# A decode kernel with w_in loaded ahead of wq, narrower moving columns at the end, and the last two rows of wo loaded 8 partitions at a time

## The chip, the cores and the metric

The kernel runs on one NeuronCore of a Trainium2 chip. The metric is device time in microseconds (us), the median of several executions. "Span" is the time from the first to the last instruction in one profiled execution; it is about 2 us shorter than the device time. Ratios are computed as the mean time of one kernel's fast runs over the mean time of the other's fast runs of the same rounds, so they are not quite the ratio of the medians quoted beside them.

Engines are named as the profile names them: PE is TensorE, PEld its weight loads, DVE VectorE, ACT ScalarE, SP SyncE. SPq and ACTq are the instruction streams of SP and ACT when they issue a DMA.

## The reference, cut to what matters

One token (x of 1024 values) goes through two blocks that are mixed by a gate:

```python
g = sigmoid((x * gate_w).sum(-1))
# A: attention of 32 query heads over 4 cached K/V heads, 65536 positions, head size 128
q = (x @ wq)                              # wq: 1024 x 4096
p = softmax(q . k_cache * 128 ** -0.5)    # k_cache, v_cache: 4 x 65536 x 128 bf16, 67 MB each
a = (p . v_cache) @ wo                    # wo: 4096 x 1024
# B: gated MLP
z = gelu(x @ w_in)                        # w_in: 1024 x 3584
b = (z1 * (w_sp * layernorm(z2) + b_sp)) @ w_out   # w_out: 1792 x 1024
out = g * a + (1 - g) * b
```

All told 162 MB are read for 2 KB of output, so this is first of all a streaming kernel.

## The kernel before: the parts that matter

Every big load goes through one helper and one pool of five 32 KB-per-partition buffers, issued by SyncE in program order. A load of a 6th tile has to wait until TensorE has finished with the tile five loads earlier.

```python
NKV = 5
WO_SPLIT = (16, 8, 4, 2, 2)     # wo's 32 row groups of 256 KB, in five loads
W = 64                          # moving columns of most score and V matmuls
WL = 128                        # moving columns of the last V group and of out_ps
...
kv = ctx.enter_context(tc.tile_pool(name="kv", bufs=NKV))
def load(src, shape, name):
    t = kv.tile([P, CT * P], BF16, name=name, tag="kv")
    ...
    nc.sync.dma_start(out=v, in_=src)
    return v
```

The order of the loads is wq (2), then K and V tiles of four heads alternating (16 + 12), then w_in's first half, V, w_in's second half, V, V, V, w_out, and wo in five pieces. The tail of the program is:

```python
z_part(0)                       # x @ w_in, first half: 112 matmuls of 18 columns
last_v(0)                       # V of the last head, tile 0: 128 matmuls of WL columns
z_part(1)
...                             # gelu, layernorm, gate: small DVE/ACT work
for j in range(1, NT):
    last_v(j)
...
def project(src, n, vec, c0, name, first=False, last=False):
    w = load(src, (n, D), name)
    for c in range(n):
        for j in range(NJ):     # NJ = 8 output blocks of 128
            nc.tensor.matmul(out_ps[j // NB][:, j % NB, :], lhsT=w[:, c, j * P:(j + 1) * P],
                             rhs=vec[:, c0 + c:c0 + c + 1].to_broadcast([P, WL]), ...)
project(B_w_out..., FC, uT, 0, "wout_t", first=True)
for n in WO_SPLIT:
    project(wo_view[:, c0:c0 + n, :], n, oa, c0, "wo_t", last=(c0 + n == OC))
    c0 += n
...                             # copy, transpose, cast, store of 2 KB
```

Moving columns are those of the operand that streams through TensorE: at full clock a matmul with 128 of them takes about 59 ns here. Only 8 of them are wanted in the scores and V matmuls (the heads of a group) and one in out_ps. The others are neighbours or copies whose products nobody reads, so their number is free.

Of the kernel before, what the change touches and what calls it, by code (L numbers as in the profile page):

```python
# [7 lines left out]
FP32 = mybir.dt.float32  # L8
BF16 = mybir.dt.bfloat16
I32 = mybir.dt.int32  # L10
ACT = mybir.ActivationFunctionType
ALU = mybir.AluOpType
AX = mybir.AxisListType

P = 128
# [3 lines left out]
CPS = 64  # L19
LAG = 4  # L20
EVAC_PAT = "vav"
WO_SPLIT = (16, 8, 4, 2, 2)
SW = 256
W = 64
WL = 128


@with_exitstack
def kernel(
# [15 lines left out]
    nc = tc.nc  # L45

    _, _, D = A_x.shape
    _, G, S, DH = A_k_cache.shape
# [3 lines left out]
    F = B_w_in.shape[1]  # L52
    FH = F // 2
    KC = D // P
    FC = FH // P
    OC = HD // P
    NJ = D // P
    QD = P // H
    NCG = S // P
    NT = NCG // CT  # L60
    SCALE = float(DH) ** -0.5
    assert DH == P and D % P == 0 and FH % P == 0 and P % H == 0
    assert S % (P * CT) == 0 and CT % CPS == 0 and CPS % TG == 0 and sum(WO_SPLIT) == OC

    const = ctx.enter_context(tc.tile_pool(name="const", bufs=1))
    wk = ctx.enter_context(tc.tile_pool(name="wk", bufs=2))
# [4 lines left out]
    pss = ctx.enter_context(tc.tile_pool(name="pss", bufs=2, space=bass.MemoryType.PSUM))  # L71
    psm = ctx.enter_context(tc.tile_pool(name="psm", bufs=1, space=bass.MemoryType.PSUM))
    pso = ctx.enter_context(tc.tile_pool(name="pso", bufs=1, space=bass.MemoryType.PSUM))


    def load(src, shape, name):
        t = kv.tile([P, CT * P], BF16, name=name, tag="kv")
        n = 1
        for s in shape:
            n *= s  # L80
        v = t[:, :n]
        if len(shape) == 2:
            v = v.rearrange("p (a b) -> p a b", b=shape[1])
        nc.sync.dma_start(out=v, in_=src)  # L84
        return v

    def load_kv(src, g, j, name):
# [9 lines left out]
    nc.scalar.dma_start(out=wb[:, 0:1], in_=B_w_sp)  # L97
    nc.scalar.dma_start(out=wb[:, 1:2], in_=B_b_sp.unsqueeze(0))

    wq_view = A_wq.rearrange("(p c) n -> p c n", c=KC)  # L100
    KH = KC // 2
    wq_t = [load(wq_view[:, i * KH:(i + 1) * KH, :], (KH, HD), "wq_t") for i in range(2)]


# [8 lines left out]
    ones_f = const.tile([P, P], FP32, name="ones_f")  # L113
# [4 lines left out]
                            op0=ALU.bitwise_and)  # L118
    nc.vector.tensor_scalar(out=pbits[:, 1:2], in0=pidx[:], scalar1=OC - 1, scalar2=None,
                            op0=ALU.bitwise_and)  # L120
    nc.vector.tensor_scalar(out=pbits[:, 2:3], in0=pidx[:], scalar1=OC.bit_length() - 1,
                            scalar2=None, op0=ALU.logical_shift_right)
# [4 lines left out]
    def one_hot(shape, dtype, in0, col, name):  # L127
# [17 lines left out]
                     start=True, stop=True)  # L145
    xm = const.tile([P, 2, KC, P // KC], FP32, name="xm")
    for t in range(2):
        nc.vector.tensor_tensor(
            out=xm[:, t], in0=xb_ps[:, t * P:(t + 1) * P].rearrange("p (i c) -> p c i", c=KC),
            in1=sel_i[:].unsqueeze(1).to_broadcast([P, KC, P // KC]), op=ALU.mult)  # L150
    xa = const.tile([P, 2, KC], FP32, name="xa")
    nc.vector.tensor_reduce(out=xa[:], in_=xm[:], axis=AX.X, op=ALU.add)
    xT = const.tile([P, KC], BF16, name="xT")
# [14 lines left out]
                            op0=ALU.add)  # L168
    nc.vector.reciprocal(out=gw[:, 2:3], in_=gw[:, 1:2])
    nc.vector.tensor_scalar(out=gw[:, 5:6], in0=gw[:, 2:3], scalar1=-1.0, scalar2=1.0,  # L170
                            op0=ALU.mult, op1=ALU.add)
    gate, wsp, bsp, gate1 = gw[:, 2:3], gw[:, 3:4], gw[:, 4:5], gw[:, 5:6]


    q_ps = psm.tile([P, H], FP32, name="q_ps", tag="m")
    for c in range(KC):
        w = wq_t[c // KH]
        for h in range(H):
            nc.tensor.matmul(  # L179
                q_ps[:, h:h + 1], lhsT=w[:, c % KH, h * DH:(h + 1) * DH], rhs=xT[:, c:c + 1],  # L180
                start=(c == 0 and h == 0), stop=(c == KC - 1), skip_group_check=True,
# [9 lines left out]
    scT, mxr, spt, o_ps, s_ps = {}, {}, {}, {}, {}  # L191
# [140 lines left out]
    while steps:  # L332
        run_step()


    win_view = B_w_in.rearrange("(p c) n -> p c n", c=KC)
    zw = 512 // (2 * FC)
    z_ps = psm.tile([P, 2 * FC, zw], FP32, name="z_ps", tag="m")

    def z_part(i):  # L340
        t = load(win_view[:, i * KH:(i + 1) * KH, :], (KH, F), "win_t")
        for c in range(KH):
            w = t[:, c, :].rearrange("p (h m f) -> p h f m", h=2, f=FC)
            for hf in range(2):
                for f in range(FC):
                    nc.tensor.matmul(  # L346
                        z_ps[:, hf * FC + f, :], lhsT=w[:, hf, f, :],
                        rhs=xT[:, i * KH + c:i * KH + c + 1].to_broadcast([P, zw]),
                        start=(i == 0 and c == 0 and hf == 0 and f == 0),
                        stop=(i == 1 and c == KH - 1), skip_group_check=True)  # L350

    def last_v(j):
        rest(v_units(G - 1, j, load_kv(A_v_cache, G - 1, j, "vt")))

    z_part(0)
    last_v(0)
    z_part(1)
    z = wk.tile([P, 2 * FC], FP32, name="z")
    nc.vector.tensor_copy(out=z[:], in_=z_ps[:, :, 0])  # L359
    gt = wk.tile([P, 2 * FC], FP32, name="gt")  # L360
    nc.vector.tensor_tensor(out=gt[:], in0=z[:], in1=z[:], op=ALU.mult)
    nc.vector.tensor_scalar(out=gt[:], in0=gt[:], scalar1=0.044715, scalar2=1.0,
                            op0=ALU.mult, op1=ALU.add)
    nc.vector.tensor_tensor(out=gt[:], in0=gt[:], in1=z[:], op=ALU.mult)
    th = wk.tile([P, 2 * FC], FP32, name="th")
    nc.scalar.activation(out=th[:], in_=gt[:], func=ACT.Tanh, scale=0.7978845608028654)
    nc.vector.tensor_scalar(out=th[:], in0=th[:], scalar1=0.5, scalar2=0.5,
                            op0=ALU.mult, op1=ALU.add)
    zg = wk.tile([P, 2 * FC], FP32, name="zg")
    nc.vector.tensor_tensor(out=zg[:], in0=z[:], in1=th[:], op=ALU.mult)  # L370
    z2 = zg[:, FC:2 * FC]
    z2sq = wk.tile([P, FC], FP32, name="z2sq")
    nc.vector.tensor_tensor(out=z2sq[:], in0=z2, in1=z2, op=ALU.mult)
    rs = wk.tile([P, 2], FP32, name="rs")
    nc.vector.reduce_sum(out=rs[:, 0:1], in_=z2, axis=AX.X)
    nc.vector.reduce_sum(out=rs[:, 1:2], in_=z2sq[:], axis=AX.X)
    tot_ps = psm.tile([P, 2], FP32, name="tot_ps", tag="m")
    nc.tensor.matmul(tot_ps[:], lhsT=ones_f[:], rhs=rs[:], start=True, stop=True)
    stat = wk.tile([P, 8], FP32, name="stat")
    nc.vector.tensor_scalar(out=stat[:, 0:2], in0=tot_ps[:], scalar1=1.0 / float(FH),  # L380
                            scalar2=None, op0=ALU.mult)
    nc.vector.tensor_tensor(out=stat[:, 2:3], in0=stat[:, 0:1], in1=stat[:, 0:1], op=ALU.mult)
    nc.vector.tensor_tensor(out=stat[:, 3:4], in0=stat[:, 1:2], in1=stat[:, 2:3],
                            op=ALU.subtract)
    nc.vector.tensor_scalar(out=stat[:, 4:5], in0=stat[:, 3:4], scalar1=1e-5, scalar2=None,
                            op0=ALU.add)
    nc.scalar.activation(out=stat[:, 5:6], in_=stat[:, 4:5], func=ACT.Sqrt)
    nc.vector.reciprocal(out=stat[:, 6:7], in_=stat[:, 5:6])
    z2n = wk.tile([P, FC], FP32, name="z2n")
    nc.vector.tensor_scalar(out=z2n[:], in0=z2, scalar1=stat[:, 0:1], scalar2=stat[:, 6:7],  # L390
                            op0=ALU.subtract, op1=ALU.mult)
    nc.vector.tensor_scalar(out=z2n[:], in0=z2n[:], scalar1=wsp, scalar2=bsp,
                            op0=ALU.mult, op1=ALU.add)
    uT = const.tile([P, FC], BF16, name="uT")
    nc.vector.scalar_tensor_tensor(out=uT[:], in0=zg[:, 0:FC], scalar=gate1, in1=z2n[:],
                                   op0=ALU.mult, op1=ALU.mult)
    for j in range(1, NT):
        last_v(j)


    NB = 512 // WL
    out_ps = [pss.tile([P, NB, WL], FP32, name="out_ps", tag="spt") for _ in range(NJ // NB)]

    def project(src, n, vec, c0, name, first=False, last=False):
        w = load(src, (n, D), name)
        for c in range(n):
            for j in range(NJ):
                nc.tensor.matmul(  # L408
                    out_ps[j // NB][:, j % NB, :], lhsT=w[:, c, j * P:(j + 1) * P],
                    rhs=vec[:, c0 + c:c0 + c + 1].to_broadcast([P, WL]),  # L410
                    start=(first and c == 0 and j % NB == 0), stop=(last and c == n - 1),
                    skip_group_check=True)


# [2 lines left out]
                     rhs=ones_f[0:1, 0:1], start=True, stop=True, skip_group_check=True)  # L417
    nc.tensor.matmul(om_ps[:, :OC], lhsT=lm[:].rearrange("p h q -> p (h q)"), rhs=sel_c[:],
                     start=False, stop=True, skip_group_check=True)
    rl = wk.tile([P, 1], FP32, name="rl")  # L420
    nc.vector.reciprocal(out=rl[:], in_=om_ps[:, OC:])
    oa = const.tile([P, OC], BF16, name="oa")
    nc.vector.tensor_scalar(out=oa[:], in0=om_ps[:, :OC], scalar1=rl[:, 0:1], scalar2=gate,
                            op0=ALU.mult, op1=ALU.mult)

    project(B_w_out.rearrange("(p c) n -> p c n", c=FC), FC, uT, 0, "wout_t", first=True)
    wo_view = A_wo.rearrange("(p c) n -> p c n", c=OC)
    c0 = 0
    for n in WO_SPLIT:
        project(wo_view[:, c0:c0 + n, :], n, oa, c0, "wo_t", last=(c0 + n == OC))  # L430
        c0 += n
    out_sb = const.tile([P, NJ], FP32, name="out_sb")
    for i, t in enumerate(out_ps):
        nc.vector.tensor_copy(out=out_sb[:, i * NB:(i + 1) * NB], in_=t[:, :, 0])  # L434
    outT_ps = psm.tile([NJ, P], FP32, name="outT_ps", tag="m")
    nc.tensor.transpose(outT_ps[:], out_sb[:], ident_f[:])
    outT = const.tile([NJ, P], BF16, name="outT")
# [4 lines left out]
    last = {}  # L442
# [37 lines left out]
```

## Time and profile before

| | before |
|---|---|
| median of 3 (later 4) runs | 398.57 us (398.07) |
| span of the profiled run | 396.6 us |
| bytes read | 162.0 MB |
| TensorE's last out_ps matmul ends | 393.4 us |

The page's strip of 40 equal slices of the span (9.9 us each; digits are busy tenths, PEclk is the granted TensorE clock, GB/s what the DMA engines moved):

```profile
PE   0435999778788787878888688896987789799997
PEclk9999999999999999999999999999999977789999
DMA  8999999999999999999999999999999999999960
GB/s 357 435 423 421 425 444 433 431 423 422 428 423 408 426 414 438 426 421 416 428 440 433 431 423 422 433 425 440 433 419 430 428 431 428 438 433 423 416 259 7
```

Up to slice 38 the DMA engines are busy all the time at about 428 GB/s, and 162 MB at that rate take 378 us. In the last quarter the clock falls for some slices, while the 18-column matmuls of z_part run and shortly after, and the PE row stands at nine up to the last slice but one.

The end of the timeline of TensorE and of what follows it (columns: start us, duration us, engine, line, operation, output<-inputs, shape, count, and in brackets the idle time before and what ended it):

```profile
337.11 6.84 PE L346 MATMUL z_ps<-xT,win_t 128*128 128x18 bf16 x112
...
351.80 1.95 PE L297 MATMUL o_ps<-scT,vt 128*128 128x128 bf16 x32
...
372.17 6.63 PE L408 MATMUL out_ps<-uT,wout_t 128*128 128x128 bf16 x112
378.63 14.96 PE L408 MATMUL out_ps<-oa,wo_t 128*128 128x128 bf16 x256
393.40 0.39 DVE L434 COPY out_sb<-out_ps 128x4 f32<-128x4 f32 x2 [20.52 <-PE out_ps L408]
394.47 0.36 SPq L439 DMA_DIRECT2D out_dram<-outT  x1
```

No wait stands in brackets on the matmul lines: the projections run back to back, 59 ns per matmul, up to 393.4 us. The DMA engines stop earlier, as the windows view of the same stretch shows (first column the stretch, then busy us of PE, PEld, DVE, ACT and POOL, then clock, DMA share and GB/s):

```profile
372.00:376.00 4.00, 4.00 (x69) 4.00 (x70) 0.48 (x2) 0.00 (x0) 0.00 (x0) 1.00 0.99 422
376.00:380.00 4.00, 4.00 (x73) 4.00 (x71) 0.00 (x0) 0.00 (x0) 0.00 (x0) 1.00 0.84 337
380.00:384.00 4.00, 4.00 (x73) 4.00 (x71) 0.00 (x0) 0.00 (x0) 0.00 (x0) 1.00 0.67 266
384.00:388.00 4.00, 4.00 (x72) 4.00 (x70) 0.00 (x0) 0.00 (x0) 0.00 (x0) 1.00 0.33 132
388.00:392.00 4.00, 4.00 (x73) 4.00 (x71) 0.00 (x0) 0.00 (x0) 0.00 (x0) 1.00 0.02 4
```

The DMA share falls from about 378 us on and is near zero from 388 us: the 16 engines do not end together. So the last 6 us belong to TensorE, and behind them, at 387 us plus about 4 us of landing and epilogue, a second limit waits: the last load.

### The profile page before, as it was taken

The page shows a single profiled execution, that of the slowest core. Times are in us where ns is not written, and L with a number is a line of the kernel's source. Part 1 is how long each engine was busy: PE and PEld are TensorE (multiplying, and loading weights), DVE is VectorE, ACT ScalarE, POOL GpSimd, SP SyncE. Part 2 cuts the span into 40 slices and gives each one's busy share as a digit, 9 for nine tenths or more (in the row PEclk, how much of TensorE's full clock was granted, in tenths as well). Part 3 has the DMA queues.
Part 4 walks back from the last instruction along what each step waited for, and adds up shares of the span by engine and source line. Part 5 has one row for each costly group of instructions (what it writes and reads, how often), then busy time and mean ns, then how long its engine had stood idle before and what let it go on. Part 6 is the DMA issues. An engine that isn't in the chain of part 4 may idle for free.

```text
span 396.6 us, 14958 instructions
## 1 busy us (share of the span) xinstructions
PE 316.6 (80%) x7080; PEld 309.1 (78%) x7080; DVE 152.7 (38%) x297; ACT 121.1 (31%) x138; POOL 1.0 (0%) x9
## 2 busy tenths in 40 slices
PE   0435999778788787878888688896987789799997
PEld 0435989777788787777878687786977689799896
DVE  2002666649344444654334346643444420110100
ACT  1002555446433233436333233553333130100000
POOL 1000000000000000000000000000000000000000
PEclk9999999999999999999999999999999977789999
DMA  8999999999999999999999999999999999999960
GB/s 357 435 423 421 425 444 433 431 423 422 428 423 408 426 414 438 426 421 416 428 440 433 431 423 422 433 425 440 433 419 430 428 431 428 438 433 423 416 259 7
DMA packets 6161, 162.96 MB, mean 411 GB/s; under 512 B 724, under 2 KB 724, under 8 KB 980
## 3 DMA queue, kind: packets, MB, share of 16 engines
q1 hardware_dynamic: 6064, 162.01, 95.7%
q8 instruction: 55, 0.90, 0.8%
q14 instruction: 6, 0.05, 0.0%
q10 hardware_dynamic: 36, 0.00, 0.0%
HBM read 162.01 MB, written 0.00 MB: 409 GB/s over the span
## 4 chain that ended last, share of the span: by engine, by line
PE 71%; DMA 13%; issue 11%; ACT 3%; DVE 1%; SPq 0%; ACTq 0%
PE tps L264 27%; PE o_ps L297 18%; PE spt L243 14%; DMA kn<-in_A_k_cache_dram 13%; PE out_ps L408 5%; PE z_ps L346 3%; PE o_ps L286 2%; ACT ktt L267 1%; ACT scT L230 1%; ACT scT L249 1%; PE nb_ps L221 0%; DVE mxr L206 0%; DVE mxr L251 0%; SPq L84 0%; DVE mx L209 0%
## 5 line engine op out<-in xcount | busy, mean ns | idle before, releaser
L264 PE MATMUL tps<-ident_b,kn 128*128 128x128 bf16 x2048 | 160.2, 222 | 19.4 <-issue 10.4
L269 DVE COPY ktt<-tps 128x1024 bf16<-128x1024 bf16 x171 | 116.8, 690 | 122.4 <-PE tps L264 122.0
L264 PEld LDWEIGHTS <-kn 128*128 128x128 bf16 x2048 | 121.9, 99 | 20.7 <-issue 13.1
L267 ACT COPY ktt<-tps 128x1024 bf16<-128x1024 bf16 x85 | 85.9, 1012 | 157.8 <-PE tps L264 157.7
L297 PE MATMUL o_ps<-scT,vt 128*128 128x64 bf16 (+1 forms) x2048 | 110.4, 203 | 14.3 <-issue 14.3
L243 PE MATMUL spt<-qT,ktt 128*128 128x64 bf16 (+7 forms) x2048 | 102.9, 192 | 17.9 <-issue 16.5
L297 PEld LDWEIGHTS <-vt 128*128 128x128 bf16 x2048 | 94.9, 100 | 16.1 <-issue 15.2
L243 PEld LDWEIGHTS <-ktt 128*128 128x128 bf16 x2048 | 84.8, 98 | 20.6 <-issue 18.7
L249 ACT CAST scT<-spt 128x512 bf16<-128x512 f32 x32 | 18.9, 589 | 24.0 <-PE spt L243 14.1
L230 ACT ACTIVATE scT<-scT 128x1024 bf16<-128x1024 bf16 x16 | 16.4, 1058 | 7.5 <-DVE scT L226 7.5
L286 PE MATMUL o_ps<-scT,ones_b 128*128 128x256 bf16 x64 | 17.8, 279 | 0.4 <-DVE ssum L308 0.3
L251 DVE TENSOR_TENSOR mxr<-scT,mxr 128x512 bf16<-128x512 bf16 x24 | 10.2, 425 | 16.5 <-ACT scT L249 15.0
L346 PE MATMUL z_ps<-xT,win_t 128*128 128x18 bf16 x224 | 13.8, 206 | 1.5 <-issue 1.5
L408 PE MATMUL out_ps<-oa,wo_t 128*128 128x128 bf16 x256 | 15.0, 219 | 0.0
L408 PEld LDWEIGHTS <-wo_t 128*128 128x128 bf16 x256 | 14.8, 98 | 0.0
L346 PEld LDWEIGHTS <-win_t 128*128 128x128 bf16 x224 | 13.7, 161 | 1.5 <-issue 1.5
L179 PE MATMUL q_ps<-xT,wq_t 128*128 128x1 bf16 x256 | 7.1, 165 | 6.9 <-DMA wq_t<-in_A_wq_dram 6.4
L179 PEld LDWEIGHTS <-wq_t 128*128 128x128 bf16 x256 | 7.1, 104 | 7.0 <-DMA wq_t<-in_A_wq_dram 6.5
L226 DVE TENSOR_TENSOR scT<-scT,negm 128x1024 bf16<-128x1024 bf16 x16 | 10.7, 685 | 0.1
L359 DVE COPY z<-z_ps 128x28 f32<-128x28 f32 x1 | 0.2, 188 | 24.4 <-PE z_ps L346 24.4
L303 DVE TENSOR_TENSOR lm<-sel_q,o_ps 128x32 f32<-128x32 f32 x4 | 0.7, 182 | 22.1 <-PE o_ps L297 22.1
L434 DVE COPY out_sb<-out_ps 128x4 f32<-128x4 f32 x2 | 0.3, 162 | 20.6 <-PE out_ps L408 20.5
(85 smaller groups left out, 52.6 us busy)
## 6 DMA issues: line engine op xcount, KB each, us to landing
kn<-in_A_k_cache_dram SPq DMA_DIRECT2D x16, 4096.0 KB, 43.2
vt<-in_A_v_cache_dram SPq DMA_DIRECT2D x16, 4096.0 KB, 27.2
wq_t<-in_A_wq_dram SPq DMA_DIRECT2D x2, 4096.0 KB, 17.4
win_t<-in_B_w_in_dram SPq DMA_DIRECT2D x2, 3584.0 KB
wo_t<-in_A_wo_dram SPq DMA_DIRECT2D x1, 4096.0 KB, 33.9
wout_t<-in_B_w_out_dram SPq DMA_DIRECT2D x1, 3584.0 KB
wo_t<-in_A_wo_dram SPq DMA_DIRECT2D x1, 2048.0 KB
wo_t<-in_A_wo_dram SPq DMA_DIRECT2D x1, 1024.0 KB
```

What stands on the lines that cost most here:

```text
L179: nc.tensor.matmul(q_ps[:, h:h + 1], lhsT=w[:, c % KH, h * DH:(h + 1) * DH], rhs=xT[:, c:c + 1], start=(c == 0 and h == 0), stop=(c == KC ...
L226: nc.vector.tensor_tensor(out=blk, in0=blk, in1=negm[:].unsqueeze(1).to_broadcast([P, CT, REP]), op=ALU.add)
L230: nc.scalar.activation(out=blk, in_=blk, func=ACT.Exp, scale=SCALE)
L243: nc.tensor.matmul(spt[g][:, o:o + n], lhsT=ktt[:, j * P:(j + 1) * P], rhs=qT[:, g * REP:g * REP + n], start=True, stop=True, skip_group_c ...
L249: nc.scalar.copy(out=blk, in_=spt[g][:].rearrange("p (c h) -> p c h", h=REP))
L264: nc.tensor.transpose(tps[:, i * P:(i + 1) * P], kn[:, u * TG + i, :], ident_b[:])
L267: nc.scalar.copy(out=ktt[:], in_=tps[:])
L269: nc.vector.tensor_copy(out=ktt[:], in_=tps[:])
L286: nc.tensor.matmul(o_ps[g][:, 2 * WL:], lhsT=ones_b[:], rhs=scT[g][:, j * CT + c:j * CT + c + SW // REP, :].rearrange("p c h -> p (c h)"), ...
L297: nc.tensor.matmul(o_ps[g][:, o0:o0 + wv], lhsT=vt[:, c, :], rhs=scT[g][:, lo:hi, :].rearrange("p c h -> p (c h)"), start=False, stop=(cg ...
L346: nc.tensor.matmul(z_ps[:, hf * FC + f, :], lhsT=w[:, hf, f, :], rhs=xT[:, i * KH + c:i * KH + c + 1].to_broadcast([P, zw]), start=(i == 0 ...
L408: nc.tensor.matmul(out_ps[j // NB][:, j % NB, :], lhsT=w[:, c, j * P:(j + 1) * P], rhs=vec[:, c0 + c:c0 + c + 1].to_broadcast([P, WL]), st ...
```

## The change

Its intent: put z_part where TensorE waits for loads anyway; make the tail's matmuls shorter (V of the last head 128 to 96 columns, out_ps 128 to 64); and split wo finer at the end, with the last two rows loaded in pieces of 8 partitions. The diff, cut to its core (the z_part code is only moved, which is marked):

```diff
-WO_SPLIT = (16, 8, 4, 2, 2)
+WO_SPLIT = (16, 8, 4, 1, 1, 1, 1)
+NARROW = 2
+NB = 8
-WL = 128
+WL = 96
-    def load(src, shape, name):
+    def load(src, shape, name, nb=P):
-        nc.sync.dma_start(out=v, in_=src)
+        for p0 in range(0, P, nb):
+            nc.sync.dma_start(out=v[p0:p0 + nb], in_=src[p0:p0 + nb])
+    win_t = [load(win_view[:, i * KH:(i + 1) * KH, :], (KH, F), "win_t") for i in range(2)]
     wq_view = A_wq.rearrange("(p c) n -> p c n", c=KC)
     ...
+    z_part(0)          # and z_part(1) and the chain to uT: moved here, ahead of q,
+    z_part(1)          # from the tail
     ...
-    out_ps = [pss.tile([P, NB, WL], FP32, name="out_ps", tag="spt") for _ in range(NJ // NB)]
+    out_ps = pss.tile([P, NJ, W], FP32, name="out_ps", tag="spt")
     ...
-                    rhs=vec[:, c0 + c:c0 + c + 1].to_broadcast([P, WL]),
+                    rhs=vec[:, c0 + c:c0 + c + 1].to_broadcast([P, W]),
     ...
-    for n in WO_SPLIT:
-        project(wo_view[:, c0:c0 + n, :], n, oa, c0, "wo_t", last=(c0 + n == OC))
+    for i, n in enumerate(WO_SPLIT):
+        project(wo_view[:, c0:c0 + n, :], n, oa, c0, "wo_t", last=(c0 + n == OC),
+                nb=NB if i >= len(WO_SPLIT) - NARROW else P)
```

More of the change, by code (lines that the diff above doesn't have):

```diff
@@ L98 @@
     nc.scalar.dma_start(out=wb[:, 1:2], in_=B_b_sp.unsqueeze(0))
+    KH = KC // 2
+    win_view = B_w_in.rearrange("(p c) n -> p c n", c=KC)
+    win_t = [load(win_view[:, i * KH:(i + 1) * KH, :], (KH, F), "win_t") for i in range(2)]
     wq_view = A_wq.rearrange("(p c) n -> p c n", c=KC)
-    KH = KC // 2
     wq_t = [load(wq_view[:, i * KH:(i + 1) * KH, :], (KH, HD), "wq_t") for i in range(2)]
@@ L172, with z_part @@
     gate, wsp, bsp, gate1 = gw[:, 2:3], gw[:, 3:4], gw[:, 4:5], gw[:, 5:6]
+    zw = 512 // (2 * FC)
+    z_ps = psm.tile([P, 2 * FC, zw], FP32, name="z_ps", tag="m")
+    def z_part(i):
+        for c in range(KH):
+            w = win_t[i][:, c, :].rearrange("p (h m f) -> p h f m", h=2, f=FC)
+            for hf in range(2):
+                for f in range(FC):
+                    nc.tensor.matmul(
+                        z_ps[:, hf * FC + f, :], lhsT=w[:, hf, f, :],
+                        rhs=xT[:, i * KH + c:i * KH + c + 1].to_broadcast([P, zw]),
+                        start=(i == 0 and c == 0 and hf == 0 and f == 0),
+                        stop=(i == 1 and c == KH - 1), skip_group_check=True)
@@ new lines @@
+    z_part(0)
+    z_part(1)
+    z = wk.tile([P, 2 * FC], FP32, name="z")
+    nc.vector.tensor_copy(out=z[:], in_=z_ps[:, :, 0])
+    gt = wk.tile([P, 2 * FC], FP32, name="gt")
+    nc.vector.tensor_tensor(out=gt[:], in0=z[:], in1=z[:], op=ALU.mult)
+    nc.vector.tensor_scalar(out=gt[:], in0=gt[:], scalar1=0.044715, scalar2=1.0,
+                            op0=ALU.mult, op1=ALU.add)
+    nc.vector.tensor_tensor(out=gt[:], in0=gt[:], in1=z[:], op=ALU.mult)
+    th = wk.tile([P, 2 * FC], FP32, name="th")
@@ new lines @@
+    nc.scalar.activation(out=th[:], in_=gt[:], func=ACT.Tanh, scale=0.7978845608028654)
+    nc.vector.tensor_scalar(out=th[:], in0=th[:], scalar1=0.5, scalar2=0.5,
+                            op0=ALU.mult, op1=ALU.add)
+    zg = wk.tile([P, 2 * FC], FP32, name="zg")
+    nc.vector.tensor_tensor(out=zg[:], in0=z[:], in1=th[:], op=ALU.mult)
+    z2 = zg[:, FC:2 * FC]
+    z2sq = wk.tile([P, FC], FP32, name="z2sq")
+    nc.vector.tensor_tensor(out=z2sq[:], in0=z2, in1=z2, op=ALU.mult)
+    rs = wk.tile([P, 2], FP32, name="rs")
@@ new lines @@
+    nc.vector.reduce_sum(out=rs[:, 0:1], in_=z2, axis=AX.X)
+    nc.vector.reduce_sum(out=rs[:, 1:2], in_=z2sq[:], axis=AX.X)
+    tot_ps = psm.tile([P, 2], FP32, name="tot_ps", tag="m")
+    nc.tensor.matmul(tot_ps[:], lhsT=ones_f[:], rhs=rs[:], start=True, stop=True)
+    stat = wk.tile([P, 8], FP32, name="stat")
+    nc.vector.tensor_scalar(out=stat[:, 0:2], in0=tot_ps[:], scalar1=1.0 / float(FH),
+                            scalar2=None, op0=ALU.mult)
+    nc.vector.tensor_tensor(out=stat[:, 2:3], in0=stat[:, 0:1], in1=stat[:, 0:1], op=ALU.mult)
@@ new lines @@
+    nc.vector.tensor_tensor(out=stat[:, 3:4], in0=stat[:, 1:2], in1=stat[:, 2:3],
+                            op=ALU.subtract)
+    nc.vector.tensor_scalar(out=stat[:, 4:5], in0=stat[:, 3:4], scalar1=1e-5, scalar2=None,
+                            op0=ALU.add)
+    nc.scalar.activation(out=stat[:, 5:6], in_=stat[:, 4:5], func=ACT.Sqrt)
+    nc.vector.reciprocal(out=stat[:, 6:7], in_=stat[:, 5:6])
+    z2n = wk.tile([P, FC], FP32, name="z2n")
+    nc.vector.tensor_scalar(out=z2n[:], in0=z2, scalar1=stat[:, 0:1], scalar2=stat[:, 6:7],
+                            op0=ALU.subtract, op1=ALU.mult)
@@ L175 @@
+    nc.vector.tensor_scalar(out=z2n[:], in0=z2n[:], scalar1=wsp, scalar2=bsp,
+                            op0=ALU.mult, op1=ALU.add)
+    uT = const.tile([P, FC], BF16, name="uT")
+    nc.vector.scalar_tensor_tensor(out=uT[:], in0=zg[:, 0:FC], scalar=gate1, in1=z2n[:],
+                                   op0=ALU.mult, op1=ALU.mult)
     q_ps = psm.tile([P, H], FP32, name="q_ps", tag="m")
@@ L333 @@
         run_step()
-    win_view = B_w_in.rearrange("(p c) n -> p c n", c=KC)
-    zw = 512 // (2 * FC)
-    z_ps = psm.tile([P, 2 * FC, zw], FP32, name="z_ps", tag="m")
-    def z_part(i):
-        t = load(win_view[:, i * KH:(i + 1) * KH, :], (KH, F), "win_t")
-        for c in range(KH):
-            w = t[:, c, :].rearrange("p (h m f) -> p h f m", h=2, f=FC)
-            for hf in range(2):
-                for f in range(FC):
-                    nc.tensor.matmul(
-                        z_ps[:, hf * FC + f, :], lhsT=w[:, hf, f, :],
-                        rhs=xT[:, i * KH + c:i * KH + c + 1].to_broadcast([P, zw]),
-                        start=(i == 0 and c == 0 and hf == 0 and f == 0),
-                        stop=(i == 1 and c == KH - 1), skip_group_check=True)
@@ L352, in last_v @@
-    def last_v(j):
-        rest(v_units(G - 1, j, load_kv(A_v_cache, G - 1, j, "vt")))
-    z_part(0)
-    last_v(0)
-    z_part(1)
-    z = wk.tile([P, 2 * FC], FP32, name="z")
-    nc.vector.tensor_copy(out=z[:], in_=z_ps[:, :, 0])
-    gt = wk.tile([P, 2 * FC], FP32, name="gt")
-    nc.vector.tensor_tensor(out=gt[:], in0=z[:], in1=z[:], op=ALU.mult)
-    nc.vector.tensor_scalar(out=gt[:], in0=gt[:], scalar1=0.044715, scalar2=1.0,
-                            op0=ALU.mult, op1=ALU.add)
-    nc.vector.tensor_tensor(out=gt[:], in0=gt[:], in1=z[:], op=ALU.mult)
@@ L365 @@
-    th = wk.tile([P, 2 * FC], FP32, name="th")
-    nc.scalar.activation(out=th[:], in_=gt[:], func=ACT.Tanh, scale=0.7978845608028654)
-    nc.vector.tensor_scalar(out=th[:], in0=th[:], scalar1=0.5, scalar2=0.5,
-                            op0=ALU.mult, op1=ALU.add)
-    zg = wk.tile([P, 2 * FC], FP32, name="zg")
-    nc.vector.tensor_tensor(out=zg[:], in0=z[:], in1=th[:], op=ALU.mult)
-    z2 = zg[:, FC:2 * FC]
-    z2sq = wk.tile([P, FC], FP32, name="z2sq")
-    nc.vector.tensor_tensor(out=z2sq[:], in0=z2, in1=z2, op=ALU.mult)
@@ L374 @@
-    rs = wk.tile([P, 2], FP32, name="rs")
-    nc.vector.reduce_sum(out=rs[:, 0:1], in_=z2, axis=AX.X)
-    nc.vector.reduce_sum(out=rs[:, 1:2], in_=z2sq[:], axis=AX.X)
-    tot_ps = psm.tile([P, 2], FP32, name="tot_ps", tag="m")
-    nc.tensor.matmul(tot_ps[:], lhsT=ones_f[:], rhs=rs[:], start=True, stop=True)
-    stat = wk.tile([P, 8], FP32, name="stat")
-    nc.vector.tensor_scalar(out=stat[:, 0:2], in0=tot_ps[:], scalar1=1.0 / float(FH),
-                            scalar2=None, op0=ALU.mult)
@@ L382 @@
-    nc.vector.tensor_tensor(out=stat[:, 2:3], in0=stat[:, 0:1], in1=stat[:, 0:1], op=ALU.mult)
-    nc.vector.tensor_tensor(out=stat[:, 3:4], in0=stat[:, 1:2], in1=stat[:, 2:3],
-                            op=ALU.subtract)
-    nc.vector.tensor_scalar(out=stat[:, 4:5], in0=stat[:, 3:4], scalar1=1e-5, scalar2=None,
-                            op0=ALU.add)
-    nc.scalar.activation(out=stat[:, 5:6], in_=stat[:, 4:5], func=ACT.Sqrt)
-    nc.vector.reciprocal(out=stat[:, 6:7], in_=stat[:, 5:6])
-    z2n = wk.tile([P, FC], FP32, name="z2n")
@@ L390 @@
-    nc.vector.tensor_scalar(out=z2n[:], in0=z2, scalar1=stat[:, 0:1], scalar2=stat[:, 6:7],
-                            op0=ALU.subtract, op1=ALU.mult)
-    nc.vector.tensor_scalar(out=z2n[:], in0=z2n[:], scalar1=wsp, scalar2=bsp,
-                            op0=ALU.mult, op1=ALU.add)
-    uT = const.tile([P, FC], BF16, name="uT")
-    nc.vector.scalar_tensor_tensor(out=uT[:], in0=zg[:, 0:FC], scalar=gate1, in1=z2n[:],
-                                   op0=ALU.mult, op1=ALU.mult)
-    for j in range(1, NT):
-        last_v(j)
@@ L401, with project @@
-    NB = 512 // WL
-    out_ps = [pss.tile([P, NB, WL], FP32, name="out_ps", tag="spt") for _ in range(NJ // NB)]
-    def project(src, n, vec, c0, name, first=False, last=False):
-        w = load(src, (n, D), name)
+    for j in range(NT):
+        rest(v_units(G - 1, j, load_kv(A_v_cache, G - 1, j, "vt")))
+    out_ps = pss.tile([P, NJ, W], FP32, name="out_ps", tag="spt")
+    def project(src, n, vec, c0, name, first=False, last=False, nb=P):
+        w = load(src, (n, D), name, nb)
         for c in range(n):
@@ L408, in project @@
                 nc.tensor.matmul(
-                    out_ps[j // NB][:, j % NB, :], lhsT=w[:, c, j * P:(j + 1) * P],
-                    rhs=vec[:, c0 + c:c0 + c + 1].to_broadcast([P, WL]),
-                    start=(first and c == 0 and j % NB == 0), stop=(last and c == n - 1),
+                    out_ps[:, j, :], lhsT=w[:, c, j * P:(j + 1) * P],
+                    rhs=vec[:, c0 + c:c0 + c + 1].to_broadcast([P, W]),
+                    start=(first and c == 0 and j == 0), stop=(last and c == n - 1),
                     skip_group_check=True)
@@ L428 @@
     c0 = 0
-    for n in WO_SPLIT:
-        project(wo_view[:, c0:c0 + n, :], n, oa, c0, "wo_t", last=(c0 + n == OC))
+    for i, n in enumerate(WO_SPLIT):
+        project(wo_view[:, c0:c0 + n, :], n, oa, c0, "wo_t", last=(c0 + n == OC),
+                nb=NB if i >= len(WO_SPLIT) - NARROW else P)
         c0 += n
     out_sb = const.tile([P, NJ], FP32, name="out_sb")
-    for i, t in enumerate(out_ps):
-        nc.vector.tensor_copy(out=out_sb[:, i * NB:(i + 1) * NB], in_=t[:, :, 0])
+    nc.vector.tensor_copy(out=out_sb[:], in_=out_ps[:, :, 0])
     outT_ps = psm.tile([NJ, P], FP32, name="outT_ps", tag="m")
```

## The prediction

> **What bounds it now.** Two resources in turn. Until about 318 us the DMA engines: the slices show about 428 GB/s in nearly every slice, and single 32 KB packets last 1.213 us with no gaps between them (16 engines x 27 GB/s = 432 GB/s). 162 MB at that rate is 375 us. From 318.7 to 393.4 us TensorE is busy almost throughout (the timeline): z_part 13.6 us in two pieces, four V tiles at 128 columns (59 ns per matmul, 7.6 us a tile; slower while the clock stands at half after the 18-column z matmuls, 113 ns), then 368 out_ps matmuls in 21.3 us. The bulk data had landed by 387.1 us; eight engines ended near 381.7 and eight near 387.1[...]. So the last 6 us and the 3.2 us of copy, transpose and store belong to TensorE.
>
> **What the change does.**
> 1. w_in first: 7.3 MB move ahead of wq. No byte fewer; every K and V tile lands about 17 us later (7.34 MB at 432 GB/s). z_part (13.6 us), its 1.5 us gap, its vector chain and the half-clock stretch after it (4 us) leave the busy tail for a start where TensorE waits for loads.
> 2. Columns: V of the last group 128 to 96 (59 to an estimated 43 ns, 8 us in all); out_ps 128 to 64, where V matmuls of 64 columns take 29 ns: 368 x 30 ns = 11 us off. Together TensorE loses over 30 us of tail and becomes idle there, so the end is now set by loads.
> 3. Two 256 KB rows become 32 loads of 8 partitions. The Trainium skill ("DMA: Bandwidth & Descriptors", Queues, rings and completion order) says such a load runs on 8 engines only, and that issue is paid per load. The trace: 128-partition issues take 0.33 us on SyncE, 8-partition ones 0.28 on ScalarE and 0.36 for the output store on SyncE. With gaps I estimate 0.31 to 0.4 us each, 10 to 13 us for 32.
>
> **The step that eats the gain.** The kv pool has five buffers. Split 16, 8, 4, 1, 1, 1, 1 makes the seventh load reuse the buffer of the 16 rows and the last that of the 8 rows. So the 32 issues can't start before TensorE has finished the 16 rows. These land near 377 us; TensorE, idle for about 6 us, starts them at half clock ("TensorE: Matmul & The Clock Gate", Part 1; here the clock dropped after idling and came back 3 to 5 us after work resumed), so they end near 382.3 to 384. Then 10 to 13 us of issuing, about 1.3 us to land (the output store took 1.2), 0.5 us of matmuls, 3 us of tail: a span of 398 to 401 against 396.6. About 30 us of TensorE time is saved and the critical path gains nothing.
>
> **Predicted time: 400.3 us, range 396.5 to 404.0.** Chances: faster by over 2%: 0.03; within 2%: 0.93; slower by over 2%: 0.04.
>
> **Checks in the profile of after.** TensorE idle between 365 and 377 and between 387 and the end; first 8-partition issue just after the last matmul of the 16-row piece; the 32 issues evenly spaced at 0.31 to 0.4 us; data rate near zero from about 387 us; the K stage shifted by 17 us with unchanged spacing; chain ending in SyncE issues and loads.
>
> **What would make it wrong.** Issues of 0.2 us (span about 394); waits between issues for loads eight earlier, adding several us; 64-column matmuls not at 29 ns; a stall of the DMA queue early, where K tiles wait for z_part.

## The result, and the profile after

| | before | after |
|---|---|---|
| median (range) | 398.07 us (397.54 to 399.08, 4 runs) | 401.99 us (401.97 to 402.35, 4 runs) |
| ratio | 1 | 1.0098, 95% interval 1.0073 to 1.0122 |
| span of the profiled run | 396.6 us | 400.5 us |
| TensorE busy | 316.6 us | 305.0 us |
| DMA packets | 6161 | 6673 |

TensorE works 11.6 us less and the kernel takes 3.9 us more. The strip of the changed kernel (slices of 10.0 us):

```profile
PE   0773389889887778959788886979795987968571
PEclk9999999999999999999999999898998799999685
DMA  8999999999999999999999999999999999999831
GB/s 333 443 425 417 437 439 426 424 432 435 425 432 430 429 428 432 425 427 432 434 429 421 432 435 425 429 430 435 421 422 445 430 421 409 428 432 430 343 126 27
```

The stream keeps its rate to the same place, but the last two slices now show 126 and 27 GB/s: the kernel goes on with almost nothing being loaded. The end of the timeline:

```profile
368.38 5.08 PE L406 MATMUL out_ps<-uT,wout_t 128*128 128x64 bf16 x112 [0.84 <-DMA wout_t<-in_B_w_out_dram]
378.05 9.77 PE L406 MATMUL out_ps<-oa,wo_t 128*128 128x64 bf16 x240 [4.59 <-DMA wo_t<-in_A_wo_dram]
391.44 0.58 PE L406 MATMUL out_ps<-oa,wo_t 128*128 128x64 bf16 x8 [3.63 <-DMA wo_t<-in_A_wo_dram]
396.87 0.58 PE L406 MATMUL out_ps<-oa,wo_t 128*128 128x64 bf16 x8 [4.84 <-DMA wo_t<-in_A_wo_dram]
397.49 0.17 DVE L432 COPY out_sb<-out_ps 128x8 f32<-128x8 f32 x1 [29.41 <-PE out_ps L406]
398.43 0.29 SPq L437 DMA_DIRECT2D out_dram<-outT  x1
```

Now each group of out_ps matmuls waits for a load, the last two groups for the two rows that come in pieces. What those loads waited for stands in the chain of waits that ended last (start us, duration us, what):

```profile
344.28 33.72 DMA wo_t<-in_A_wo_dram
378.05 6.30 PE out_ps L406 x128
384.37 0.35 SPq L87
384.77 0.28 SPq L87
...
394.61 0.29 SPq L87
394.94 1.58 DMA wo_t<-in_A_wo_dram
396.52 0.35 issue
396.87 0.60 PE out_ps L406 x8
```

It is to be read from top to bottom. The 16-row piece of wo lands at 378.0 us. TensorE takes 6.30 us for its 128 matmuls, 49 ns each, and at the moment when these are done SyncE issues the first 8-partition load, into the buffer that the 16 rows had. From the first issue at 384.37 to the last at 394.94 there are 31 intervals, so 0.341 us per issue. 1.9 us after the last issue begins, the last eight matmuls start. SyncE, which carries no data, is the critical engine for 10.9 us. The windows view shows that TensorE and the DMA engines both have little to do there, and that TensorE had been granted half a clock when the rows came:

```profile
376.00:380.00 4.00, 1.95 (x37) 1.96 (x38) 0.00 (x0) 0.00 (x0) 0.00 (x0) 0.55 0.66 278
380.00:384.00 4.00, 4.00 (x90) 4.00 (x88) 0.00 (x0) 0.00 (x0) 0.00 (x0) 0.60 0.48 199
388.00:392.00 4.00, 0.56 (x8) 0.45 (x8) 0.00 (x0) 0.00 (x0) 0.00 (x0) 0.75 0.18 49
392.00:396.00 4.00, 0.03 (x1) 0.00 (x0) 0.00 (x0) 0.00 (x0) 0.00 (x0) 0.50 0.19 49
```

The theory to be tested: the columns turn TensorE's tail into slack; moving w_in adds slack to slack; and the 32 issues, which may only start late, cost more than the columns gave. Its rivals: the small loads are slow because they use half of the engines; the cost comes from the later K and V; the cost is the half clock; the whole fault is the wait for the buffer.

### The profile page after: what moved, and what is told of

It reads as the page before. It is cut to its first block, busy times and chain, and to the rows that moved or that the text cites. A ratio compares the mean times of both kernels' runs of the same rounds, so it can differ in the third digit from the quotient of the medians.

```text
span 400.5 us, 15001 instructions
## 1 busy us (share of the span) xinstructions
PE 305.0 (76%) x7080; PEld 295.1 (74%) x7080; DVE 152.3 (38%) x296; ACT 122.5 (31%) x139; POOL 1.0 (0%) x9
## 2 busy tenths in 40 slices
DMA packets 6673, 162.97 MB, mean 407 GB/s; under 512 B 980, under 2 KB 980, under 8 KB 1492
## 4 chain that ended last, share of the span: by engine, by line
PE 52%; DMA 32%; issue 9%; SPq 3%; ACT 2%; DVE 1%; ACTq 0%
PE tps L325 26%; DMA kn<-in_A_k_cache_dram 23%; PE spt L304 13%; PE o_ps L358 10%; DMA wo_t<-in_A_wo_dram 9%; SPq L87 3%; PE out_ps L406 2%; PE o_ps L347 1%; ACT scT L291 1%; ACT ktt L328 1%; ACT scT L310 0%; ACT L291 0%; PE nb_ps L282 0%; DVE mxr L267 0%; ACTq L473 0%
## 5 line engine op out<-in xcount | busy, mean ns | idle before, releaser
L325 PE MATMUL tps<-ident_b,kn 128*128 128x128 bf16 x2048 | 163.5, 224 | 26.6 <-issue 13.9
L325 PEld LDWEIGHTS <-kn 128*128 128x128 bf16 x2048 | 123.2, 100 | 30.0 <-issue 16.7
L358 PE MATMUL o_ps<-scT,vt 128*128 128x64 bf16 (+1 forms) x2048 | 101.2, 197 | 13.1 <-issue 10.8
L358 PEld LDWEIGHTS <-vt 128*128 128x128 bf16 x2048 | 85.3, 99 | 15.7 <-issue 12.4
L304 PEld LDWEIGHTS <-ktt 128*128 128x128 bf16 x2048 | 85.2, 99 | 13.6 <-issue 12.3
L406 PE MATMUL out_ps<-oa,wo_t 128*128 128x64 bf16 x256 | 10.9, 214 | 13.1 <-DMA wo_t<-in_A_wo_dram 13.1
L406 PEld LDWEIGHTS <-wo_t 128*128 128x128 bf16 x256 | 10.6, 112 | 13.4 <-DMA wo_t<-in_A_wo_dram 8.4
L347 PEld LDWEIGHTS <-ones_b 128*128 128x128 bf16 x64 | 6.4, 99 | 2.3 <-issue 1.6
```

What stands on the lines that cost most here:

```text
L304: nc.tensor.matmul(spt[g][:, o:o + n], lhsT=ktt[:, j * P:(j + 1) * P], rhs=qT[:, g * REP:g * REP + n], start=True, stop=True, skip_group_c ...
L325: nc.tensor.transpose(tps[:, i * P:(i + 1) * P], kn[:, u * TG + i, :], ident_b[:])
L347: nc.tensor.matmul(o_ps[g][:, 2 * WL:], lhsT=ones_b[:], rhs=scT[g][:, j * CT + c:j * CT + c + SW // REP, :].rearrange("p c h -> p (c h)"), ...
L358: nc.tensor.matmul(o_ps[g][:, o0:o0 + wv], lhsT=vt[:, c, :], rhs=scT[g][:, lo:hi, :].rearrange("p c h -> p (c h)"), start=False, stop=(cg ...
L406: nc.tensor.matmul(out_ps[:, j, :], lhsT=w[:, c, j * P:(j + 1) * P], rhs=vec[:, c0 + c:c0 + c + 1].to_broadcast([P, W]), start=(first and ...
```

## The experiments

All gave correct results. Medians are of device time; the kernel before ran beside each (397.85 to 398.61 us). Spans are of the profiled run.

| run | what differs | median us | ratio to before | span us |
|---|---|---|---|---|
| after | the change | 401.99 | 1.0098 | 400.5 |
| e1_wide | after, last two rows as wide loads | 394.54 | 0.9903 | 393.1 |
| e2_nb16 | after, 16 partitions per small load | 399.57 | 1.0037 | 397.1 |
| e3_order | before, w_in first only | 397.90 | 0.9997 | 395.8 |
| e4_narrow | before, small loads only | 405.94 | 1.0193 | 401.8 |
| e5_cols | before, columns only | 392.88 | 0.9864 | 391.1 |
| e6_order_cols | columns and w_in first | 393.06 | 0.9868 | 391.3 |
| e7_own_narrow | after, one-row pieces in own buffers | 401.94 | 1.0091 | 400.1 |
| e8_own_wide | e7 with wide loads | 393.38 | 0.9879 | 391.5 |
| e9_pre_narrow | four rows early, 16 loads of 8 partitions | 406.11 | 1.0177 | 402.5 |
| e10_pre_wide | four rows early, one wide load | 393.73 | 0.9879 | 391.8 |
| e13_two_queues | after, small loads from SP and ACT in turn | 399.60 | 1.0018 | 398.6 |
| e14_pre_nb16 | e9 with 8 loads of 16 partitions | 404.34 | 1.0163 | 402.5 |

### e1_wide: the changed kernel without the small loads

```diff
-NARROW = 2
+NARROW = 0
```

> The changed kernel with the last two rows of wo loaded by one 128-partition load each; order, columns and split stay. Issue theory (32 issues one after another on SyncE, 0.34 us each, starting only when TensorE has finished the 16 rows): 30 issues go, the first of the two last loads is issued near 384.4 us and the second when the 8 rows are done, near 386.3 us; both land by about 388.5, span 391 to 393, ratio to the kernel before 0.985 to 0.99. Rival, the moved w_in (K lands 17 us later) costs the time: the span stays near 400. Rival, the cold clock of TensorE in the tail costs it: the span stays within 2 us of 400.

Measured: span 393.1 us, ratio 0.9903. The issue theory's range (391 to 393) was missed by 0.1 us in the profiled run and met by the other three (392.1 to 392.8), the ratio was missed by next to nothing; both rivals named there are out, since w_in is still first and TensorE still starts the 16 rows at half clock (granted 0.50 from 376 to 380 us and 0.69 from 380 to 384). 30 issues less are worth 7.4 us of span. The last row's load is issued at 386.1 us, when the 8 rows are done, and its matmuls start 3.5 us later:

```profile
378.14 9.68 PE L406 MATMUL out_ps<-oa,wo_t 128*128 128x64 bf16 x248 [4.78 <-DMA wo_t<-in_A_wo_dram]
389.63 0.42 PE L406 MATMUL out_ps<-oa,wo_t 128*128 128x64 bf16 x8 [1.81 <-DMA wo_t<-in_A_wo_dram]
```

I had allowed 2.2 us for that; it is why this run is at the top of the range.

### e2_nb16: half as many small loads

```diff
-NB = 8
+NB = 16
```

> The changed kernel with the last two rows loaded by DMAs of 16 partitions each: 16 issues in place of 32, and each load can use 16 DMA engines in place of 8. Issue theory: the cost is proportional to the count, so 16 x 0.34 = 5.4 us less than the changed kernel, span 395 to 396, ratio to before about 0.997. Rival, the loads are slow because they use only half of the engines: nearly all of the loss goes, span near 392.

Measured: span 397.1 us, ratio 1.0037 (1.0005 to 1.0070). Neither number was hit. The rival (half of the engines) does not explain it: these loads use all 16 engines (see "Eight engines" below), and yet 4.0 us of the 7.4 us between the changed kernel and e1_wide remain. What was gained, 3.4 us of span (2.4 us of the medians), is about what the train of issues got shorter: 7.4 us from first to last in place of 10.6. But "proportional to the count" was too simple as well. In the trace's records an 8-partition issue on SyncE lasts 0.29 us and the next begins 0.34 us after it; a 16-partition issue lasts 0.42 us and the next begins 0.46 us after it. One of the 16 issues took 0.93 us for no reason that the trace shows. So back to back a 16-partition issue cost more than an 8-partition one; that the cost grows with the partitions in general is not shown, and a lone wide issue in the tail is recorded at 0.33 us.

### e3_order: w_in first and nothing else

```diff
+    win_t = [load(win_view[:, i * KH:(i + 1) * KH, :], (KH, F), "win_t") for i in range(2)]
     wq_t = [...]
     ... # z_part and its chain moved ahead of q; WL = 128, WO_SPLIT = (16, 8, 4, 2, 2) as before
```

> The kernel before with w_in first and nothing else (128 columns, split 16, 8, 4, 2, 2, all loads 128 partitions). If the tail is bound by TensorE from the landing of the 16 rows on (32 rows x 8 x 59 ns = 15.1 us from about 378.1 us), nothing is gained: TensorE ends at 393 to 394 us when the clock is full, span 396 to 397; up to 3 us more if it starts the rows at half clock after idling. Rival, the order alone takes z_part's 13 us off the critical path: span about 390 or less. Rival, the order is what costs the 4 us: span 400.

Measured: span 395.8 us, ratio 0.9997 (0.9965 to 1.0028); the expected range was 396 to 397, and the four runs have spans of 395.7 to 397.5. 13.6 us of TensorE work left the tail and nothing came of it:

```profile
369.30 6.63 PE L407 MATMUL out_ps<-uT,wout_t 128*128 128x128 bf16 x112
377.86 14.97 PE L407 MATMUL out_ps<-oa,wo_t 128*128 128x128 bf16 x256 [1.93 <-DMA wo_t<-in_A_wo_dram]
```

The 16 rows land near 378 us whatever the order of loads, as no byte is saved; behind them stand 256 matmuls at 59 ns. Before the change TensorE reached them at 378.6 us without a pause; now it reaches them early, waits 1.93 us and starts at 377.9 us. The order is neither a gain nor the loss.

### e4_narrow: the kernel before with the small loads only

```diff
-WO_SPLIT = (16, 8, 4, 2, 2)
+WO_SPLIT = (16, 8, 4, 1, 1, 1, 1)    # and load(..., nb=8) for the last two pieces
```

> The kernel before with only the split 16, 8, 4, 1, 1, 1, 1 and the last two rows in 8-partition loads. Issue theory: the 32 issues start when the 16 rows are done, near 386.1 us at 59 ns per matmul, take 10.9 us, the last lands near 398.5, span 402 to 403, ratio about 1.014. Rival, the issues hide behind the TensorE tail that lasts to 393.4 us anyway: span 397 to 399.

Measured: the profiled run has a span of 401.8 us, and the first issue comes at 385.27, the last at 395.82: the train of 32 again, and not hidden by TensorE's longer tail. The median of four runs is 405.94 us (403.84 to 408.37), the profiled run being the fastest. The profiled run agrees with the theory to 0.2 us. The other three have spans of 403.2 to 406.5 us, above its range; they have no trace, and these up to 4.7 us more stay unexplained.

### e5_cols and e6_order_cols: columns without and with the moved w_in

```diff
-WL = 128
+WL = 96                              # e5: the kernel before with this
-    out_ps = [pss.tile([P, NB, WL], ...) for _ in range(NJ // NB)]
+    out_ps = pss.tile([P, NJ, W], ...)   # W = 64; e6: also w_in first
```

> The kernel before with only the narrower columns (96 in the last V group, 64 in out_ps); w_in stays late, split 16, 8, 4, 2, 2, wide loads. If TensorE's surplus in the tail is what the columns remove, TensorE waits for the 16 rows (land near 377 to 378 us) and then for the last row pair, which lands near 387.1 as in the kernel before: TensorE ends near 387.8, span 390.5 to 391.5, ratio 0.983 to 0.988. Rival, z_part in the tail still holds TensorE back: span 394 or more.

> The changed kernel with split 16, 8, 4, 2, 2 and wide loads, that is columns plus w_in first. Loads bind the tail: the last lands near 387, span 390.5 to 391.5. If moving w_in adds nothing once the columns are narrow, this equals the run with columns alone within 0.5 us; if it adds what it takes from the tail, it is 2 us or more faster than that run.

Measured: spans 391.1 and 391.3 us, ratios 0.9864 and 0.9868. Columns alone give the whole gain that any version here reached, 5.5 us of span, and w_in first adds nothing to it. These are the best two versions, 1.4% below the kernel before. In e5 TensorE waits for loads before all the projections, so what binds is the landing of the last piece:

```profile
367.88 5.08 PE L407 MATMUL out_ps<-uT,wout_t 128*128 128x64 bf16 x112 [0.99 <-DMA wout_t<-in_B_w_out_dram]
377.73 9.51 PE L407 MATMUL out_ps<-oa,wo_t 128*128 128x64 bf16 x240 [4.78 <-DMA wo_t<-in_A_wo_dram]
387.44 0.67 PE L407 MATMUL out_ps<-oa,wo_t 128*128 128x64 bf16 x16 [0.20 <-DMA wo_t<-in_A_wo_dram]
```

The half clock at the head of the 240 matmuls costs nothing here: they are done 0.2 us before the last load lands.

### e7_own_narrow and e8_own_wide: is it only the wait for the buffer?

```diff
+    kvs = ctx.enter_context(tc.tile_pool(name="kvs", bufs=4))
-        t = kv.tile([P, CT * P], BF16, name=name, tag="kv")
+        if n == D_OWN:     # 1024: the four one-row pieces
+            t = kvs.tile([P, n], BF16, name=name, tag="kvs")
+        else:
+            t = kv.tile([P, CT * P], BF16, name=name, tag="kv")
# e8: NARROW = 0 as well
```

> The changed kernel with the four one-row pieces of wo in four buffers of their own, so the 8-partition loads no longer wait until TensorE has finished the 16 and the 8 rows. If the wait for the buffer is the whole cause, the 32 issues are done by 370 us and the span is near 391. But each load also waits for the load eight before it (eight completion semaphores in rotation): then only about seven get out before 385 us and some 25 issues of 0.34 us follow, the last lands near 395.5, span 398 to 399.5, only 1 to 2 us less than the changed kernel.

> As the run before, but the four one-row pieces are wide loads: no buffer wait and no issue train. All four are issued before 387 us is near; the last lands with the bulk at about 387, span 390 to 391.5. Against the run with wide loads in the shared pool (span 393.1) the difference of about 2 us is what the wait for the buffers costs alone.

Measured: e7 has a span of 400.1 us, e8 of 391.5. Three of the four runs of the changed kernel have 400.1 us too (the profiled one 400.5), and the medians are 401.94 and 401.99 us: freeing the buffers gave the small loads nothing that can be told from noise, less even than the 1 to 2 us expected. It also settles the half clock: in e7 no small load waits for TensorE, and the time is the same. The records of SyncE show what holds the small loads instead. There are eight completion semaphores (counters that tell that a load has landed), used in turn, and each issue first waits until the load that used its semaphore eight loads before has landed (start ns, duration ns, what it waits for and what it signals):

```
357584 347 DMA                signals semaphore=109     first 8-partition load
359684 283 DMA waits S[110]>= signals semaphore=110
368136 272 DMA waits S[100]>= signals semaphore=100     S[100]: w_out has landed
377811 272 DMA waits S[101]>= signals semaphore=101     S[101]: the 16 rows
382641 271 DMA waits S[102]>= signals semaphore=102     S[102]: the 8 rows
385128 272 DMA waits S[103]>= signals semaphore=103     S[103]: the 4 rows
```

Eight small loads got out by 386.4 us; the other 24 followed from 386.7 us on at 0.338 us each:

```profile
386.36 0.27 SPq L92
386.63 0.04 issue
386.68 0.29 SPq L92
...
394.11 0.29 SPq L92
394.45 1.56 DMA wo_t<-in_A_wo_dram
```

In e8 the same buffers hold wide loads: all four are issued by 359.8 us. Against e1_wide (393.1) the buffers alone are worth 1.6 us of span, 1.2 us of the medians. So the wait for the buffer costs the wide loads a little and the small ones nothing, because their other wait, for the semaphores, ends as late. The changed kernel's own records agree: its eighth small load is issued at 386.79 us, and the load whose semaphore it needs had landed only at 386.55. From there on it is the issues alone that set the pace: in the second half of the train each issue comes about 1.1 us after its semaphore was free. The number of semaphores was not varied, so this wait is read from the records and not tested by a run of its own.

### e13_two_queues: the same loads issued by two engines

```diff
+            eng = nc.scalar if nb < P and (p0 // nb) % 2 else nc.sync
-            nc.sync.dma_start(out=v[p0:p0 + nb], in_=src[p0:p0 + nb])
+            eng.dma_start(out=v[p0:p0 + nb], in_=src[p0:p0 + nb])
```

> The changed kernel with every other one of the 32 8-partition loads issued by ScalarE, which is idle there; count, size, engines and buffers stay as they were. If the cost is the time one sequencer needs per issue (0.34 us each on SyncE alone), each queue issues 16 in 5.4 us: the last lands near 391, span near 395, ratio about 0.997. If the cost lies in what both queues share (generating the descriptors, completing small loads, eight completion semaphores), the rate of issues does not double and the span stays at 398 to 400.5.

Measured: span 398.6 us (the other three runs 396.9 to 398.2), median 399.60 us, 2.4 us less than the changed kernel, between the two theories and nearer to the second. The 32 issues take 8.8 us in place of 10.9:

```profile
384.32 8.84 SPq L88 DMA_DIRECT2D wo_t<-in_A_wo_dram  x16
384.32 8.61 ACTq L88 DMA_DIRECT2D wo_t<-in_A_wo_dram  x16
```

The records show two causes. Up to 388.5 us only 11 loads get out: some wait for loads of the bulk, and one issue on each queue takes 1.2 us, for no reason that the trace shows. From 389.7 us on a load goes out every 0.20 us, not every 0.17, and the same semaphore comes round every 1.6 to 1.8 us. Nearly all of these issues start about 20 ns after the load that used their semaphore before has landed: with eight loads allowed in flight, the time that one small load needs from issue to completion now sets the pace. The Trainium skill, "DMA: Bandwidth & Descriptors", Issuing engines are not separate DMA queues, says that issuing from several engines only saves the sequencer's issue time. This run agrees, and shows that here even that saving is mostly lost to another limit.

### e9_pre_narrow, e10_pre_wide and e14_pre_nb16: small loads out of the tail

If issues in the tail are the fault, 8-partition loads issued early might still be used to shift work to DMA engines that end early.

```diff
-WO_SPLIT = (16, 8, 4, 1, 1, 1, 1)
+WO_SPLIT = (16, 8, 2, 2)
+PRE = 4
     def load_kv(src, g, j, name):
+        kv_n[0] += 1
+        if kv_n[0] > 6 and pre_parts:
+            p0 = pre_parts.pop(0)      # NB = 8 in e9, 128 in e10, 16 in e14
+            nc.sync.dma_start(out=wo_pre[p0:p0 + NB], in_=wo_view[p0:p0 + NB, OC - PRE:, :])
```

> Columns and w_in first as in the changed kernel; the last four rows of wo (1 MB) have a buffer of their own and are loaded during the K and V stage by 16 loads of 8 partitions and 8 KB each, one beside each of 16 big loads, so that no issue lies in the tail; the rest is split 16, 8, 2, 2, wide. If 8-partition loads run on the eight DMA engines that end early (near 378 us in the other runs, the other eight near 387), 1 MB moves to these: the late eight end 2.4 us earlier, near 384.7, span 388.5 to 389.5, about 2 us less than the wide twin of this run. If they run on the late engines, the span is 2 us longer than the twin's. If the engine makes no difference: equal.

> The twin: the same four rows loaded early by one 128-partition load. No byte leaves the late engines, so the last load still lands near 387 and the span is 390.5 to 391.5, as with the columns alone.

> The run with four rows loaded early by 16 loads of 8 partitions had a span of 402.5 in place of the hoped 389: its last loads landed near 398 and its 32 KB packets got longer (533 of 4480 over 1.3 us, 61 in the wide twin). Here the same rows come early by 8 loads of 16 partitions. If the cause there was that 8-partition loads put all bytes on eight engines, some of them the late ones, so that engines drift apart, 16-partition loads spread evenly: long packets near 70, span 391 to 392.5. If small loads among the big ones are the cause whatever their engines, long packets stay in the hundreds and the span is 396 or more.

Measured: e10 has a span of 391.8 us, 0.3 us above the top of its range. e9 and e14 have 402.5 us each, with no small issue in the tail. All three expectations for e9 are refuted, and for e14 the second holds. The windows view of e9, then of e10, in the middle of the stream, where no tail plays a part:

```profile
100.00:160.00 60.00, 47.87 (x1160) 46.16 (x1157) 29.67 (x51) 26.17 (x30) 0.00 (x0) 1.00 1.00 412
180.00:240.00 60.00, 46.58 (x1063) 45.30 (x1059) 26.02 (x47) 21.82 (x24) 0.00 (x0) 0.91 1.00 404
```

```profile
100.00:160.00 60.00, 50.02 (x1204) 48.03 (x1202) 31.30 (x54) 27.01 (x31) 0.00 (x0) 1.00 1.01 430
180.00:240.00 60.00, 49.61 (x1202) 48.38 (x1199) 28.13 (x49) 23.30 (x26) 0.00 (x0) 0.97 1.01 431
```

The DMA engines are busy in both, but in e9 they move 4 to 6% less. The records of single packets say how: a 32 KB packet of a K or V tile lasts 1.213 us as a rule; of 4480 such packets, 61 lasted over 1.3 us in e10, 533 in e9 and 497 in e14. They lie between 80 and 260 us in e9 and between 80 and 200 us in e14, that is, around the stretch in which the small loads were in the stream (their packets run from 97 to 262 us and from 97 to 181 us). So a few small loads among big ones cost the big ones time, with 8 and with 16 partitions alike. Both runs load 128 small packets, and both have about 3.5 more long packets than the twin for each of them (472 and 436); the twin has the same 128 packets in one load, between 97 and 102 us, and no such rise. Why they do it is open. No run has several small loads of 128 partitions in the stream, so it is not shown either that the few partitions matter and not merely the number of separate loads.

## Why the prediction was right, point by point

- **The size and the sign.** Predicted 400.3 us (396.5 to 404.0), measured 401.99; predicted span 398 to 401, measured 400.5. Against the middle of the predicted spans 1.0 us is missing: the first issue came 1.2 us after the middle of its range, the train from first to last issue (10.6 us) was 0.9 us shorter than the middle of its own, and landing took 0.6 us more. For the step from span to device time it allowed 0.8 us, where 1.5 us lie between the profiled span and the median.
- **What bound the kernel before.** Right. e3_order shows the tail limited by the 16 rows' landing plus 256 matmuls, e5_cols shows that shortening these matmuls uncovers the next limit, the last landing, 5.5 us lower. The forecast for 64 columns held as well: 29 to 30 ns, measured 31.
- **w_in first.** Right that K and V would shift by 17 us without harm (the first matmul on K starts at 33.7 us before and at 51.1 after). The prediction summed it up with the columns as "over 30 us of tail"; e3_order and e6_order_cols show more exactly that this part is worth nothing, alone or with the columns.
- **The buffer chain.** Right, and visible in the chain of waits: the first small issue at 384.37 us, when the 128 matmuls that began at 378.05 us and took 6.30 us are done (predicted: from near 377 to 382.3 to 384). But the total does not confirm this step, and in that the prediction had some luck: e7_own_narrow, without the buffer chain, takes the same time, because the eight completion semaphores hold most of the issues as long. The prediction had these only among the things that could make it wrong.
- **The issues.** Predicted 0.31 to 0.4 us each and 10 to 13 us in all, measured 0.34 and 10.9. From the last issue to the last matmuls it was 1.9 us, where 1.3 to land had been allowed.
- **The half clock.** Right in part. The Trainium skill, "TensorE: Matmul & The Clock Gate", Part 1, says that an idle stretch of about 3.4 us puts TensorE at half clock and that about as much work brings it back. The windows show 0.55 and 0.60 between 376 and 384 us, and the 128 matmuls took 49 ns each. TensorE had stopped at 373.5 us; the granted clock fell in the window from 376 to 377 us (0.68), near the page's figure, and was back only in that from 383 to 384 us (0.90), about 5 us after work resumed, later than the page's figure. What the prediction said of the clock in the kernel before does not hold for all drops there: one came in the window from 342 to 344 us (0.66), after 5 us of back-to-back 18-column matmuls. TensorE was not idle from 365 to 377 us, as forecast, but worked 5 us for w_out in between. The clock is not the cause of the loss: e1_wide has nearly the same clock (the first issue comes 6.0 us after its rows, in place of 6.3) and is 7.4 us faster, e6_order_cols starts its rows at half clock too (0.50 from 376 to 380 us) and reaches 391.3, and in e7_own_narrow the small loads do not wait for TensorE at all and nothing is gained.
- **Eight engines.** The Trainium skill, "DMA: Bandwidth & Descriptors", Why a DMA increments its semaphore by 16 and not by 1, says that a load issued by SyncE runs on the largest number of engines up to 16 that divides the slowest dimension of both its access patterns, so on 8 for 8 partitions, and that each of them ends with a write to the semaphore. The profiles agree with the rule: against e1_wide, packets under 512 B rise from 756 to 980 in the changed kernel and in e2_nb16, by 224 in both, which is 32 x 8 - 2 x 16 and 16 x 16 - 2 x 16. e2_nb16 shows that the number of engines was not what cost time. The prediction's statement that eight engines ended near 381.7 us and eight near 387.1 came from following packets from one to the next in the trace; the falling DMA share in the windows fits it. The reason that it gave, instruction fetches, was argued only and tested by no run.

## What to carry to other kernels

Count the DMA issues that can only start after the last big load's buffer or semaphore is free, and multiply: at a third of a microsecond each, the 32 issues here took 10.9 us, more than the 5.5 us that the columns alone had won. Work taken off an engine counts only up to the next limit, which here was the landing of the last load 5.5 us below; so look for that limit first, then choose the smallest change that reaches it (here the columns alone, ratio 0.986). Load the end of a stream in few wide pieces, each into a buffer that is free early.

## What the Trainium skill lacked or had wrong

- "DMA: Bandwidth & Descriptors" has no issue cost for a load from SyncE by its shape (only one per instruction, for the generations before trn3). Back to back the runs show 0.34 us per load for 8 partitions and 0.46 us for 16 (2 KB per partition).
- The same page, Issuing engines are not separate DMA queues, calls the issue time "usually small relative to the DMA itself". For a train of 8-partition loads of 16 KB it is not what to reckon with: 0.34 us of issue each, against packets of 0.08 us that run side by side. One load alone takes 1.6 us from issue to landing, but up to eight are in flight, and the issues set the pace.
- No page says that separate small loads (of 8 or 16 partitions here) slow the big loads around them: 533 and 497 of 4480 packets over 1.3 us where the wide twin has 61, and 404 GB/s in place of 431.
- "TensorE: Matmul & The Clock Gate", Back-to-back issue gap, gives about 81 ns per matmul for weight load and matmul pairs at 128 columns. The projections of the kernel before ran at 58 ns a pair (256 in 14.96 us).
